# A gated dilated convolution on one core: another list of instructions, with one accumulating transfer fewer and four output evictions more on VectorE

## The chip, the cores and the metric

The kernel runs on one core of a Trainium2 chip. The metric is the device time of one execution in microseconds (us); the profile's span is the part of it between the first and the last recorded event of the core. Five engines work side by side and meet only through semaphores: TensorE multiplies matrices (PE in the profile, PEld for its weight loads), VectorE (DVE) and ScalarE (ACT) do elementwise work and can read the matrix products out of PSUM, GpSimd (POOL) does elementwise work on SBUF and issues transfers that add to what lies at their target, and SyncE (SP) issues the other transfers. Each engine takes its own instructions strictly in the order in which they were written.

## The reference

```python
x: (2, 16000, 256)   w: (3, 256, 512)   w_o: (256, 256)      # all bf16
xp = jnp.pad(x, ((0, 0), (4, 0), (0, 0)))                    # causal, dilation 2
h  = x @ w[0] + (x two steps back) @ w[1] + (x four steps back) @ w[2]
f, g = h[..., :256], h[..., 256:]
z  = jnp.tanh(f) * sigmoid(g)
return z @ w_o
```

So there is a convolution with three taps over time, a gate, and a projection.

## The kernel before

**Tiling.** Channels lie on the partitions. The 32000 time steps are cut into 23 groups. A group reads its piece of x through a transposing transfer into a tile `xt`, in which time is split into 4 or 6 phases, so that the dilation of two turns into neighbouring pairs of phases. There are three kinds. Group 0 (kind P) is computed straight from the taps, to have work while the rest is loaded. The four groups of kind B (4 phases) use the short-convolution trick that gets two pairs of outputs from four products instead of six; its operands are `m`, `p`, `d0`, `d3`, sums and differences of pairs of phases. The eighteen groups of kind A (6 phases) get three pairs of outputs from five products; their operands start as `u1`, `e`, `f`, `u0`, `u2` (each a sum or difference of pairs of phases), and four of them are finished by adding a multiple of `u1`: `rm` is e + `u3`, `rp` is f + `u1`, `r0` is u0 + `uh`, `ri` is u2 + `ud`, where `u3`, `uh`, `ud` are scaled copies of `u1`. An operand tile is 128 partitions by 1024 elements in bf16 (640 where the group has 160 rows).

**Blocks.** A block is one group with one quarter of the 512 outputs. There are 88, in the order of `ORDER`. A block of kind A runs: the first product (token `F`) into a PSUM bank `b`; ScalarE copies it to `ss` (`c`); the middle product is added (`M`); a copy of the bank scaled against `ss` goes to `hh`, on VectorE (`h`) or plainly on ScalarE (`k`); the last product is added (`L`); VectorE makes from `ss` and `b` the start of a second bank `a` (`A`) and, from `hh`, the middle pair `yy` (`Y`); two more products land on the banks (`Z` on `b`, `I` on `a`); ScalarE applies tanh or sigmoid to `b`, `yy` and `a` (`b`, `y`, `a`). Kind B has no `M`, `h`, `Y`. Bank `b` exists three times, bank `a` twice. All products of a block are two matmuls on line 359. When tanh and sigmoid of a half are there, VectorE multiplies them (`g`, lines 456 and 460), and the projection of 128 rows by two phases is four matmuls on line 478 (`P`). Its bank (three of them) is evicted to the output tile `osb` by ScalarE (`e`, line 495) or VectorE (`v`, line 487), and SyncE stores a finished `osb` (`s`). The pieces of the last group are projected in two halves (`H`, `R`).

**Who makes the operands.** A token such as `u2.10` names an operand and the number of its group. Bare, it is one VectorE instruction (line 330, or 328 for the scaled copies). With a `d` behind it, GpSimd issues a transfer that adds the scaled copy to the operand in place (line 325): an accumulating DMA of 256 KB. With a `q` and a number, it is a quarter of the operand as one GpSimd instruction of 256 elements per partition (160 for the narrow group); four such tokens make the operand. The number says behind which of VectorE's latest instructions the piece is held.

```python
if "q" in token:
    on_gpsimd(token)
elif token[-1] == "d":
    pre(*group_of(token[:-1]), None)
...
    note(pre(*group_of(token), nc.vector))
...
elif what in "ev":
    out_evict(*pieces[int(token[1:])], on_v=what == "v")
```

**What sets the order.** `PLAN` is one list of all tokens behind the start-up. The program walks it and writes every instruction to its engine's queue, without any reordering. An engine's order is therefore the order of its tokens in the list, and where a token of one engine stands between two tokens of another tells what is meant to start when. Waits follow from the data and from the buffers.

Of the kernel before, what the change touches and what calls it, by code (L numbers as in the profile page):

```python
# [34 lines left out]
A f.6q22 b P s11 uh.5 M a u2.5q82 Y F y rp.5d u0.5 P k16 Z e.6 e27 r0.5d L b g I c P u2.6q118 A y F M e28 u1.6q63 Y
P c f.6q1 h17 Z y I ud.5 e29 rm.5 M b s12 L h18 a u2.6q1 x F a P u2.6q45 A c L Y u1.6q20 e30 I A u1.6q108 e31 M Z a
Y u1.6q33 P k19 g ri.5d Z b L e32 u0.6 P f.7q89 y A I b F uh.6 u2.6q46 e33 P Y c F r0.6d u3.6 P y g rm.6d M e34 I
f.6q13 a h20 P c Z y u1.7 L f.6q67 b M A e35 P rp.6d Y F k21 s14 P a e.7 s13 Z c ud.6 I g e36 ri.6d L b M u2.7q71 A
e37 P a h22 F u0.7q137 e38 P Y u0.7q65 c L s15 Z y uh.7 x u2.7q72 A M b I f.7q90 h23 e39 F f.7q1 y Y L c f.7q114 I
v40 a Z u2.7q22 Y a M g P b P k24 A F e41 x L rp.7 e42 P c A Z y u1.8 I u0.8q93 b M Y a P u0.7q161 h25 Z y F uh.8 b  # L40
u3.7 I u2.8 s16 c rm.7d F e43 f.8 M c L g rp.8d k26 M a u2.7q76 A L k27 Y I y u0.8q1 A Z a u0.7q103 P v44 b u0.8q81
L Y y s17 P u0.8q162 A e45 F r0.7d e46 Z ud.7 Y c I ri.7d P b u3.8 r0.8d M u1.9 a Z e.8 k28 F b ud.8 L rm.8d e.9 c I
y g F u2.9q179 M y A P c P e47 h29 f.9q46 M a Y s18 f.9q43 L e48 s1 ri.8 u2.9q60 Z x k30 I A b L u2.9q117 Y a F y
u0.9q14 A Z c I g u0.9q1 b P a M Y F y u0.9q167 h31 I e49 ud.9 Z c u3.9 L b e.10 rm.9d M e50 A P u0.9q89 a F s19 h32
e51 I x Y f.9q75 c P g L a f.9q1 Z e52 Y P b M u0.10q72 A e53 F u1.10 Z c I h33 y P uh.9 b M f.10 s20 r0.9d y L h34
u2.9q136 F e54 A P a L c Y u0.10q111 I y Y u0.10q129 M e55 Z A rp.9d k35 P uh.10 ri.9d b Z g a I L e56 ud.10 u3.10 F
b s21 A P a x F u2.10 c P Y c M y u1.11 Z e57 M h36 b I u3.11 e58 L g u2.11q137 k37 F P a A L y Y u2.11q107 P c A
u2.11q42 Z y I f.11 rm.10d y M Y b u0.10q118 P e59 v60 rp.10d Z k38 s22 F uh.11 r0.10d b g P a L u0.11 c F P e61 A I
e62 ud.11 ri.10q1 M c Y P y r0.11d u1.12 Z y rp.11d M h39 b I e.11 e63 L u3.12 a F ri.10q1 h40 P e64 A P c ri.10q52
L e65 Y u2.11q33 M a s24 g ri.10q10 Z k41 x I b A L a F u2.12q103 Y y I u2.12q220 A c Z uh.12 rm.11d P y Y P b g M y  # L50
s23 F k42 v66 I u1.13q121 c Z v67 a ri.11d L f.12 e68 M b P A s25 e.13q152 P k43 x Y F a e.13q125 L c e.12 u1.13q170
Z e69 A I b M f.13 u1.13q1 e70 P Y a F u2.12q52 P v71 k44 Z c rp.12d g L y rm.12d M b A I k45 ud.12 P u2.13q69 Y a
s26 F e72 u0.12 L u2.13q15 c Z A P y u2.13q63 M Y b I u1.13q210 e73 h46 F a u2.12q15 Z c uh.13 rp.13d I g y L ri.12d
b M ud.13 P A k47 e.14q113 F a Y L c e.13q247 I A y Z e.14q191 e74 M Y e.13q189 P b h48 Z r0.12d y u3.13 F a g L
rm.13d b I f.14 c P u2.14q103 y F A e75 M v76 u0.13q202 I c h49 P u0.13q57 e77 M Y a u2.14q55 s28 L e78 h50 x
u0.13q102 Z a Y P u2.13q15 b L A e.14q70 y P y F u1.14 u0.13q101 Z A c I b ri.13d Y M e79 s27 F r0.13d u3.14 k51 g Z
c I u1.15 a L M b A f.15q131 P a u3.15 F f.15q226 e80 Y P k52 s29 e.15 P c x L g e81 Z y M A u0.15q78 b I h53
e.14q248 P y F Y e82 u2.15q170 L a u0.14 u2.15q128 Z c P Y b I u2.15q278 A e83 M rm.14d a ud.14 F h54 e84 Z rp.14d
uh.14 I c g L r0.14d b P e85 u2.14q287 A M y P Y e86 P h55 u2.14q38 y F u1.16 a Z ri.14d I g b L c P Y f.16q41 e87 F
e88 A M f.16q231 c P h56 u0.15q120 e89 Z v90 M a f.15q216 s32 L b s30 h57 u0.15q75 I x y A f.16q213 F a L Y f.15q45  # L60
y P uh.15 u0.15q94 c Z A e91 I s31 u2.15q110 Y M b P rm.15d g a F k58 rp.15d Z u3.16 c uh.16 L y u2.16 M b I ud.15 A
k59 P ri.15d F a ud.16 r0.15d Y L y P d0.3q55 c A Z e92 M Y b I u1.17 e93 d0.3q1 Z a h60 I m.3q93 b F e.16 ri.16d L
c g F rm.16d y P e.17q121 A c M e94 P h61 e95 M e.17q79 Y I a s34 f.16q22 L h62 s33 a Z A e96 d3.3q1 P y d0.3q64 Y P
e.17q45 b L g Z y rp.16d F b d3.3q40 Y I c P d3.3q65 A e97 F m.3q78 u0.16 e98 d0.3q252 M c I s35 h63 r0.16d Z a
u3.17 M e99 f.17 P b h64 L rp.17d a P A y u0.17q176 F e100 Y L y P d3.3q161 A u0.17q101 c Z Y I e.17q58 b I e101 g M
rm.17d a F s36 u2.17q5 h65 y P s4 s7 Z c g p.3q78 s5 L b M A e102 P u0.17q112 k66 Y F u2.17q17 a P v104 c L m.3q26
uh.17 p.3q67 Z e103 A M p.3q36 b s37 ud.17 I m.3q10 k67 Y P u0.17q286 a F v106 p.3q135 y L r0.17d Z c A P u2.17q16 y
M Y b I u2.17q30 e105 h68 Z a v107 F ri.17q5 b L ri.17q4 s38 y I A ri.17q3 P c Y F y ri.17q28 M c g Z a P h69 b P g
e108 M L e109 h70 F y I A c P a Y L I y Y Z a A M b P h71 y Z v110 F b L c I A F a L Y P c A I e113 v111 Z a L v112
Z b P A b s40 I g y s39 P a F I v114 c F P g c L a Z e115 A L P v116 b I e117 A Z s41 P g a s6 I b v118 Z a P b P  # L70
e119 g H P v120 s42 R P e121 H e123 v122 H R s44 R e124 s43 e125 s45
"""


# [572 lines left out]
```

## Time and profile before

| | |
|---|---|
| time, median of 3 runs | 258.87 us (258.47 to 259.78) |
| the profiled execution's own time | 258.77 us |
| its span | 256.6 us |
| TensorE busy | 249.9 us (97%), 1428 matmuls |
| VectorE busy | 242.8 us (95%), 405 instructions |
| ScalarE busy | 243.7 us (95%), 492 instructions |
| GpSimd busy | 176.9 us (69%), 249 instructions |

Each share of busy time says less than it seems. A matmul's recorded time reaches past the start of the next one, and so does that of a VectorE or ScalarE instruction: back to back, they start sooner after each other than each of them lasts. To see what an engine's work costs it, one has to read the distance between the starts of neighbours, and to see its waits, the places where that distance is longer than usual. The groups of instructions ("lines"), the chain of work that ended last, and the timeline in order of time are the views used below; a time at the start of a timeline row is us from the span's start, the second number is the us that the row lasts, and xN counts merged instructions.

### The profile page before, as it was taken

Reading aid. Unit: us, or ns where it says so; the run is one execution under the profiler, and the core shown is the slowest. Engines: PE = TensorE matmul, PEld = TensorE weight load, DVE = VectorE, ACT = ScalarE, POOL = GpSimd, SP = SyncE. Lnnn points to the kernel's source line nnn. Section 1 sums busy time; section 2 is a strip of 40 time slices with the busy share of each in tenths; the row PEclk is TensorE's granted clock in tenths of the full one; section 3 lists DMA queues with packets and bytes.
Section 4 is the critical chain, followed back from the end, with each engine's and each line's share of the span. In section 5 each row is a group of like instructions: output and inputs, shape, how many; then the busy total and the mean of one; then the engine's idle time right before and its main releaser. Section 6 shows DMA issues by size and latency. Waiting matters only on the chain.

```text
span 256.6 us, 4575 instructions
## 1 busy us (share of the span) xinstructions
PE 249.9 (97%) x1428; PEld 138.0 (54%) x1428; DVE 242.8 (95%) x405; ACT 243.7 (95%) x492; POOL 176.9 (69%) x249
## 2 busy tenths in 40 slices
PE   8999999999999999999999999999999999999992
PEld 4655555555555565545555555555555545555581
DVE  2999999999999999999999999999999999999991
ACT  4988999999999999999999999999999999999893
POOL 1064554997699888499764887999798798897000
PEclk9999999999999999999999999999999999999997
DMA  6999979989989899999999999996999998773054
GB/s 184 213 202 213 196 172 159 232 143 203 187 199 271 187 200 249 182 289 200 200 237 212 249 196 188 290 244 147 212 260 171 216 219 224 198 217 102 0 226 176
DMA packets 84320, 51.73 MB, mean 202 GB/s; under 512 B 69032, under 2 KB 70312, under 8 KB 84296
## 3 DMA queue, kind: packets, MB, share of 16 engines
q1 hardware_dynamic: 74168, 33.71, 54.3%
q0 software_dynamic: 9216, 16.78, 37.7%
q10 hardware_dynamic: 912, 0.95, 1.1%
q8 instruction: 11, 0.18, 0.3%
q14 instruction: 13, 0.11, 0.1%
HBM read 1.25 MB, written 16.38 MB: 69 GB/s over the span
## 4 chain that ended last, share of the span: by engine, by line
PE 82%; DVE 8%; DMA 3%; ACT 2%; issue 2%; ACTq 0%; DVEq 0%
PE b L359 48%; PE o_ps L478 18%; PE a L359 13%; DVE a L393 2%; DMA e<-u 2%; DVE zz L460 2%; DVE yy L393 2%; PE b L379 1%; PE a L379 1%; DMA xn<-in_x_dram 1%; DVE hh L393 1%; ACT osb L495 1%; ACT sg L441 1%; ACT th L441 0%; ACT ss L390 0%
## 5 line engine op out<-in xcount | busy, mean ns | idle before, releaser
L330 POOL TENSOR_TENSOR u<-xt 128x256 bf16<-128x256 bf16 x88 | 66.8, 774 | 15.0 <-PE b L359 8.4
L478 PE MATMUL o_ps<-wo_sb,zz 128*128 128x256 bf16 x496 | 72.0, 273 | 0.0
L495 ACT CAST osb<-o_ps 128x512 bf16<-128x512 f32 x101 | 63.8, 646 | 0.9 <-PE o_ps L478 0.7
L478 PEld LDWEIGHTS <-zz 128*128 128x128 bf16 x496 | 48.5, 98 | 27.6
L393 DVE SCALAR_TENSOR_TENSOR a<-ss,b 128x512 f32<-128x512 f32 (+1 forms) x88 | 59.5, 679 | 2.3 <-PE b L359 1.3
L390 ACT COPY ss<-b 128x512 f32<-128x512 f32 (+1 forms) x88 | 55.0, 628 | 0.9 <-PE b L359 0.6
L359 PEld LDWEIGHTS <-w_sb 128*128 128x128 bf16 x352 | 34.1, 97 | 35.1 <-issue 3.0
L359 PE MATMUL b<-e,wm_sb 128*128 128x512 bf16 x144 | 42.8, 379 | 0.3 <-DMA e<-u 0.3
L359 PE MATMUL b<-u,w_sb 128*128 128x512 bf16 x144 | 42.9, 379 | 0.2
L359 PE MATMUL b<-u,wa_sb 128*128 128x512 bf16 x144 | 42.9, 379 | 0.0
L359 PE MATMUL b<-f,wp_sb 128*128 128x512 bf16 x144 | 42.9, 379 | 0.0
L359 PE MATMUL a<-u,w_sb 128*128 128x512 bf16 x144 | 42.5, 379 | 0.3 <-DVE a L393 0.2
L460 DVE TENSOR_TENSOR zz<-th,sg 128x1536 bf16<-128x1536 bf16 (+2 forms) x46 | 41.3, 897 | 0.2
L441 ACT ACTIVATE th<-b 128x512 bf16<-128x512 f32 (+1 forms) x44 | 28.0, 636 | 1.4 <-ACT ss L390 0.7
L441 ACT ACTIVATE th<-a 128x512 bf16<-128x512 f32 (+1 forms) x44 | 28.6, 649 | 0.3 <-PE a L359 0.2
L441 ACT ACTIVATE sg<-b 128x512 bf16<-128x512 f32 (+1 forms) x44 | 28.0, 635 | 0.6 <-PE b L359 0.5
L441 ACT ACTIVATE sg<-a 128x512 bf16<-128x512 f32 (+1 forms) x44 | 28.3, 642 | 0.0
L359 PEld LDWEIGHTS <-wm_sb 128*128 128x128 bf16 x176 | 17.0, 98 | 17.2 <-DMA e<-u 1.2
L359 PEld LDWEIGHTS <-wp_sb 128*128 128x128 bf16 x176 | 16.9, 98 | 17.3 <-issue 1.6
L393 DVE SCALAR_TENSOR_TENSOR hh<-ss,b 128x512 f32<-128x512 f32 x38 | 25.9, 681 | 0.2
L393 DVE SCALAR_TENSOR_TENSOR yy<-hh,b 128x512 f32<-128x512 f32 x38 | 25.6, 678 | 0.0
L441 ACT ACTIVATE sg<-yy 128x512 bf16<-128x512 f32 x36 | 24.9, 693 | 0.7 <-DVE yy L393 0.7
(68 smaller groups left out, 373.2 us busy)
## 6 DMA issues: line engine op xcount, KB each, us to landing
out_dram<-osb SPq DMA_DIRECT2D x36, 384.0 KB, 3.5
u<-uh POOLq DMA_DIRECT2D x18, 256.0 KB, 4.8
f<-u POOLq DMA_DIRECT2D x16, 256.0 KB, 4.7
u<-ud POOLq DMA_DIRECT2D x15, 256.0 KB, 4.6
e<-u POOLq DMA_DIRECT2D x15, 256.0 KB, 4.8
out_dram<-osb SPq DMA_DIRECT2D x8, 256.0 KB, 3.1
w_sb<-in_w_dram ACTq DMA_DIRECT2D x3, 256.0 KB, 4.1
xt<-in_x_dram SPq DMA_TRANSPOSE x22, 8.0
```

The costliest lines, as they stand in the source:

```text
L330: ins = eng.tensor_tensor(out=o, in0=a, in1=b, op=op)
L359: nc.tensor.matmul(G[bank, oi][:, :2 * R], lhsT=wmat[:, ct, osl], rhs=G[mv][:, :, ct, :R], start=which == "first" and ct == 0, stop=ct == ...
L379: nc.tensor.matmul(G[bank, oi][:, :4 * r].rearrange("p (j r) -> p j r", j=4), lhsT=w_taps[tap][:, ct, osl], rhs=xt[:, j0:j0 + 4, ct, c0 + ...
L390: nc.scalar.copy(out=G["ss", oi][:, :n], in_=G["b", oi][:, :n])
L393: return note(nc.vector.scalar_tensor_tensor(out=out, in0=in0, scalar=scalar, in1=in1, op0=ALU.mult, op1=op))
L441: nc.scalar.activation(out=G[name, dt][:, j:j + 2, :R], in_=G[bank, oi][:, :2 * R].rearrange("p (q r) -> p q r", q=2), func=(ACT.Tanh, ACT ...
L460: note(nc.vector.tensor_tensor(out=G["z"][:, dt, :, :n], in0=G["th", dt][:, :, :n], in1=G["sg", dt][:, :, :n], op=ALU.mult))
L478: nc.tensor.matmul(o_ps[:, q, :], lhsT=z, rhs=wo_sb[:, dt, :], start=dt == 0 and (q == 0 or len(dts) == NT), stop=dt == NT - 1, skip_group ...
L495: copy(out=G["osb", at][:, 2 * jp:2 * jp + 2, :], in_=o_ps[:])
```

## The change

Only `PLAN` is changed, and all of it: 1730 tokens before and after, in another order, with these exchanges. Nothing else in the file differs, and the order of the blocks, of the groups and of each product kind is the same.

```diff
-m.0 d3.0 p.0 F F d0.0 c F c G L w L A c D wa.5q2 D A wa.2q5 Z d0.1 I b D m.1 a L wa.3q1 F d A wa.10q2 Z c p.1 I
+m.0 p.0 d3.0 F F d0.0 c D c D G L w L A D wa.5q2 F A wa.6q6 d I c d0.1 Z a m.1 Z b L G b I A wa.4q1 F a d3.1 F c Z
...
-e119 g H P v120 s42 R P e121 H e123 v122 H R s44 R e124 s43 e125 s45
+a Z s41 v118 I b P g a Z P v119 b P e120 g s42 P v121 H H e122 H R R s43 v123 R e124 v125 s44 s45
```

| what | before | after |
|---|---|---|
| output evictions on ScalarE / VectorE (`e` / `v`) | 103 / 23 | 99 / 27 |
| `hh` on VectorE / ScalarE (`h` / `k`) | 38 / 34 | 37 / 35 |
| accumulating transfers (`d`) | 64 | 63 |
| operand instructions on VectorE of line 330 | 74 | 75 |
| scaled copies on VectorE (`u3`, `uh`, `ud`) | 54 | 54 |
| quarter pieces on GpSimd (with the 16 of the weights, `wa`) | 176 | 176 |

Operand by operand: `u2.10` and `u2.16` go from VectorE to GpSimd; `d3.2`, `d0.3` and `d3.3` from GpSimd to VectorE (the last two belong to the narrow group); `ri.8` and `rp.7` from VectorE to a transfer; `rp.12` and `r0.0` from a transfer to VectorE; `rm.7` and `r0.17` from a transfer to GpSimd; `ri.17` from GpSimd to a transfer.

VectorE, where the third group of four phases (its `xt` is `xt_145`) is prepared, some 12 us behind the start of the list. Before:

```order
L330 TENSOR_TENSOR m_397<-xt_145 128x1024
L393 SCALAR_TENSOR_TENSOR a_407<-ss_352,b_345 128x512
L393 SCALAR_TENSOR_TENSOR a_416<-ss_389,b_376 128x512
L330 TENSOR_TENSOR u0_422<-xt_143 128x1024
L328 TENSOR_SCALAR u3_430<-u1_350 128x1024
L330 TENSOR_TENSOR u2_436<-xt_143 128x1024
L330 TENSOR_TENSOR p_440<-xt_145 128x1024
```

The same place in the changed list:

```order
L330 TENSOR_TENSOR d3_402<-xt_145 128x1024
L330 TENSOR_TENSOR m_411<-xt_145 128x1024
L330 TENSOR_TENSOR d0_422<-xt_145 128x1024
L393 SCALAR_TENSOR_TENSOR a_428<-ss_386,b_377 128x512
L393 SCALAR_TENSOR_TENSOR a_440<-ss_409,b_398 128x512
L328 TENSOR_SCALAR ud_451<-u1_361 128x1024
```

The difference `d3` of this group, four GpSimd pieces before, is now a VectorE instruction ahead of `m`, and `d0` has come up behind it.

GpSimd's last instructions, which make the last operands of the last group of six phases (u0, u2) and of the narrow group (m, p). Before:

```order
L330 TENSOR_TENSOR u0_3180<-xt_2697 128x256
L330 TENSOR_TENSOR p_3241<-xt_2886 128x160
L325 DMA u0_3180<-uh_3280 128x1024
L330 TENSOR_TENSOR u2_3224<-xt_2697 128x256 x2
L330 TENSOR_TENSOR u2_3224<-u2_3224,ud_3294 128x256 x4
```

After:

```order
L325 DMA u2_3161<-ud_3270 128x1024
L330 TENSOR_TENSOR u0_3210<-xt_2722 128x256
L330 TENSOR_TENSOR m_3282<-xt_2856 128x160
L330 TENSOR_TENSOR u0_3210<-xt_2722 128x256
L330 TENSOR_TENSOR u0_3210<-u0_3210,uh_3276 128x256 x4
```

The sum onto u2 (`ri.17`) has become a transfer, and the sum onto u0 (`r0.17`) four quarter pieces, the last work of GpSimd.

ScalarE's last instructions; `osb` and `odd` are output tiles, `th` and `sg` results of tanh and sigmoid. Before:

```order
L441 ACTIVATE sg4_3589<-b_3533 128x2x160
L495 CAST osb6_3564<-o_ps_3591 128x512
L495 CAST osb6_3612<-o_ps_3607 128x512
L493 CAST odd_3625<-o_ps_3605 128x256
L495 CAST osb4_3636<-o_ps_3622 128x512
L495 CAST osb4_3636<-o_ps_3628 128x512
```

After:

```order
L441 ACTIVATE sg4_3592<-a_3561 128x2x160
L441 ACTIVATE sg4_3592<-b_3536 128x2x160
L495 CAST osb6_3608<-o_ps_3596 128x512
L495 CAST osb6_3608<-o_ps_3613 128x512
L495 CAST osb4_3636<-o_ps_3621 128x512
```

The eviction of `odd` and the second one of `osb4` have left ScalarE. VectorE's last instructions, before:

```order
L487 CAST osb6_3564<-o_ps_3571 128x512
L456 TENSOR_TENSOR zo_3577<-th4_3580,sg4_3589 128x128
L460 TENSOR_TENSOR zz_3576<-th4_3580,sg4_3589 128x4x128
L487 CAST osb6_3612<-o_ps_3597 128x512
L487 CAST osb6_3612<-o_ps_3616 128x512
```

After:

```order
L456 TENSOR_TENSOR zo_3589<-th4_3574,sg4_3592 128x128
L460 TENSOR_TENSOR zz_3588<-th4_3574,sg4_3592 128x4x128
L487 CAST osb6_3608<-o_ps_3603 128x512
L487 CAST odd_3632<-o_ps_3619 128x256
L487 CAST osb4_3636<-o_ps_3625 128x512
```

So the last two evictions of all, one behind the other on ScalarE before, are now on two engines.

More of the change, by code (lines that the diff above doesn't have):

```diff
@@ new lines @@
+e10 rm.1 Z c f.3q18 A P b u1.3q12 M Y y F r0.1d g k4 Z c I e.2 b M a u2.2 L rm.2d e11 F h5 u1.3q6 e12 I A r0.2d P c
+u3.3 L a Y M y f.2 Z u0.3q1 e13 P A x b I g k6 u0.3q30 F a L Y c I f.3q30 A y P Z a f.3q46 Y M e14 rp.2d e.3 Z b
+ri.2d I ud.3 k7 v15 F b L u1.4 c F uh.3 y u0.3q1 P A a M u3.4 u0.3q32 c P Y P k8 rm.3d g y Z r0.3d L e18 v16 M b
+f.4q43 I A k9 F v17 a L f.3q70 c Y P s8 y u2.4q60 A Z y u2.4q5 I Y b M rp.3d e.4 e19 Z a F h10 rm.4d b I u2.3 L c
+u1.5 F x f.4q1 a M A c P g k11 e.5q65 M y L Y k12 P u2.4q3 A e20 I e21 L f.4q7 Y Z a ri.3d f.5 P b I u0.4 y Z
@@ new lines @@
+F y I u0.8q26 A c M e47 P Y f.9q43 e48 M s18 h29 a u2.9q86 x Z k30 L e.9 u0.9q32 b I A y L f.9q76 Y F a I g c u2.9q1
+Z e49 M A b P r0.8d h31 a P s17 u2.9q24 y Y F L e50 u1.10 Z c u2.9q170 s19 I A b M f.9q120 Y y P e51 f.9q93 h32 F y
+Z e.10 rp.9d L c u3.9 P b g rm.9d M a F u0.10q73 e52 h33 P c A I u0.9q36 e53 L Y a M u0.10q117 s20 Y e54 Z x
+u2.10q47 h34 y P u0.9q156 I b A L y g F a P c uh.9 Z u2.10q1 Y e55 M u0.9q113 b A I k35 P e.11 r0.9d y Z f.10 L a
+ud.9 F b A ri.9d I c u3.10 F rp.10d a Y M c P uh.10 e56 h36 Z e57 M g s21 I b x L k37 u1.11 u2.11q202 F a A P c L
@@ new lines @@
+e80 Z e81 I s29 u0.15q25 A P b x h53 P a u2.15q101 F Y e82 u2.14q72 L c P u0.15q136 Y e83 M u2.14q144 y A Z y
+u2.15q123 I h54 Z b rp.14d u0.14 L a g F b r0.14d I c f.15q226 Y F a P A c M u0.15q126 v84 y Z u2.14q105 y I h55 P b
+ri.14d u3.15 M u1.16 e85 F e86 g L c s31 P A f.16q308 k56 x P e87 ud.15 M f.16q283 Y a I e88 f.15q157 L h57 a Z
+u2.15q239 A L b u2.15q168 P s30 Y e89 F u0.15q166 v90 y Z f.16q155 c A P b I f.15q155 Y M y rm.15d g F k58 rp.15d I
+c u1.17 Z a L u0.16 b M A P k59 uh.15 F e91 d0.3 r0.15d L Y a P ri.15d c P A u2.16q18 y Z Y M e92 I b v93 s33
@@ L72 @@
+ri.17d e106 L u0.17q34 e107 Z A c P s38 m.3q64 Y b I u0.17q8 M y Z y r0.17q14 h68 I a r0.17q9 F b g L r0.17q27 c P
+e108 A F M r0.17q95 Y c I y h69 M a Z h70 P b g L y L a A F P Y c I A y Z Y M e109 I b h71 Z a v110 F b L c P A y F
+L Y c I e111 v112 P a Z v113 a L P A b s40 P A y s39 Z g F b I c P g a F I c v114 L a Z A L e115 P A b I e116 v117 P
+a Z s41 v118 I b P g a Z P v119 b P e120 g s42 P v121 H H e122 H R R s43 v123 R e124 v125 s44 s45
 """
```

79 lines of the change are left out of this document (31 added, 48 removed).

## The prediction, made before the changed kernel was run

> **What bounds the kernel now.** I read the first page and the chain of waits, then counted each engine's work by lines, then looked in the timeline at the places where TensorE starts late.
>
> ```profile
> span 256.6 us, 4575 instructions
> PE 249.9 (97%) x1428; PEld 138.0 (54%) x1428; DVE 242.8 (95%) x405; ACT 243.7 (95%) x492; POOL 176.9 (69%) x249
> PE 82%; DVE 8%; DMA 3%; ACT 2%; issue 2%; ACTq 0%; DVEq 0%
> ```
>
> The chain runs on TensorE for 82% of the span, and VectorE is next. TensorE's work is best told from the distance of its starts:
>
> ```profile
> 40.28 1.29 PE b L359 x6
> 46.04 0.87 PE o_ps L478 x8
> 11.20:251.70 240.50, 201.85 (x848) 81.99 (x848) 1.00 0.95 202
> 11.20:251.70 240.50, 72.42 (x500) 48.84 (x500) 1.00 0.95 202
> 11.30 1.46 PE L359 MATMUL b<-m,wm_sb 128*128 128x512 bf16 x6
> 250.20 1.47 PE L478 MATMUL o_ps<-wo_sb,zz 128*128 128x256 bf16 x12
> ```
>
> A product matmul costs 1.29/6 = 0.215 us in the chain, a projection matmul 0.87/8 = 0.109. The two window rows count them (the first is line 359, the second line 478): 848 x 0.215 = 182.3, less 32 narrow ones of 320 instead of 512 columns at, by their size, 0.08 less each, 2.6, plus 500 x 0.109 = 54.5, plus six matmuls of the start group, 0.8: 235.0 us. From 11.30 to 251.67 there are 240.4. So TensorE loses some 4 to 5 us in all behind its start. That is the most that a better list could win there, and what a worse one makes larger. Two of the losses:
>
> ```profile
> 110.86 0.59 PE L359 MATMUL b<-f,wp_sb 128*128 128x512 bf16 x2
> 110.89 0.69 DVE L393 SCALAR_TENSOR_TENSOR a<-ss,b 128x512 f32<-128x512 f32 x1
> 111.49 0.68 DVE L393 SCALAR_TENSOR_TENSOR yy<-hh,b 128x512 f32<-128x512 f32 x1
> 111.63 0.59 PE L359 MATMUL a<-u,w_sb 128*128 128x512 bf16 x2 [0.18 <-DVE a L393]
> 112.22 0.59 PE L359 MATMUL b<-u,w_sb 128*128 128x512 bf16 x2
> 201.43 5.33 DMA e<-u
> 205.88 0.59 PE L359 MATMUL b<-u,w_sb 128*128 128x512 bf16 x2
> 206.81 0.61 PE L359 MATMUL b<-e,wm_sb 128*128 128x512 bf16 x2 [0.34 <-DMA e<-u]
> ```
>
> Two product matmuls take 0.43, so the pair behind 110.86 was due at 111.29. It starts at 111.63, right when VectorE's `a` ends at 111.58; the next pair was due at 112.06 and starts at 112.22, when `yy` ends. The pair due at 206.31 starts at 206.81, because an accumulating transfer issued at 201.43 took 5.33. Late VectorE is the frequent case, a late transfer the large one.
>
> **VectorE's margin.** The same count for VectorE; the five window rows are lines 393, 330, 328, 460 and 487, in this order:
>
> ```profile
> 9.20:252.60 243.40, 127.76 (x198) 1.00 0.95 202
> 9.20:252.60 243.40, 50.57 (x74) 117.65 (x160) 1.00 0.95 202
> 9.20:252.60 243.40, 23.62 (x54) 1.00 0.95 202
> 9.20:252.60 243.40, 41.26 (x46) 1.00 0.95 202
> 9.20:252.60 243.40, 15.56 (x23) 1.00 0.95 202
> 9.23 0.69 DVE L330 TENSOR_TENSOR m<-xt 128x1024 bf16<-128x1024 bf16 x1
> 9.84 0.69 DVE L330 TENSOR_TENSOR d<-xt 128x1024 bf16<-128x1024 bf16 x1
> 22.81 0.42 DVE L328 TENSOR_SCALAR uh<-u 128x1024 bf16<-128x1024 bf16 x1
> 23.14 0.69 DVE L330 TENSOR_TENSOR m<-xt 128x1024 bf16<-128x1024 bf16 x1
> 23.75 1.28 DVE L393 SCALAR_TENSOR_TENSOR a<-ss,b 128x512 f32<-128x512 f32 x2
> 242.55 1.28 DVE L487 CAST osb<-o_ps 128x512 bf16<-128x512 f32 x2
> 244.15 0.95 DVE L460 TENSOR_TENSOR zz<-th,sg 128x1536 bf16<-128x1536 bf16 x1
> 245.02 0.68 DVE L487 CAST osb<-o_ps 128x512 bf16<-128x512 f32 x1
> 250.84 0.69 DVE L487 CAST osb<-o_ps 128x512 bf16<-128x512 f32 x1 [0.27 <-PE o_ps L478]
> ...
> L460 DVE TENSOR_TENSOR zz<-th,sg 128x1536 bf16<-128x1536 bf16 x36 | 35.5, 985 | 0.2
> ```
>
> Start to start, a sum of 1024 elements costs 9.84 - 9.23 = 0.61, a scaled copy 0.33, a step on a bank 1.28 - 0.69 = 0.60 (rounded), an eviction 1.28 - 0.68 = 0.60, a gate of 1536 elements 0.87. That gives 198 x 0.60 = 118.8, 74 x 0.61 = 45.1, 54 x 0.33 = 17.8, 46 gates of which 36 are large at 0.87 and ten smaller at about 0.5 by their size, 36.3, and 23 x 0.60 = 13.8: 231.8 us. From 9.23 to 251.53 there are 242.3. About 10.5 us, 4%, are waits and stretched instructions, and little of it is free in the middle:
>
> ```profile
> 53.00:105.00 52.00, 51.93 (x293) 28.43 (x292) 51.43 (x85) 51.94 (x106) 42.90 (x59) 1.00 0.99 207
> 105.00:157.00 52.00, 51.65 (x285) 27.48 (x284) 51.98 (x90) 51.77 (x104) 38.93 (x49) 1.00 1.09 214
> ```
>
> (Windows: length, then busy time of TensorE, its weight loads, VectorE, ScalarE, GpSimd.) VectorE is busy 51.43 and 51.98 of 52 us. It is a second bound, hardly behind TensorE.
>
> **The change part by part.** *VectorE's total.* Four evictions more, 4 x 0.60 = +2.4; one `hh` less, -0.6; one 1024-wide sum fewer (u2.10, u2.16, ri.8 and rp.7 go, d3.2, rp.12 and r0.0 come), -0.6; two narrow differences more (d0.3, d3.3, 640 elements: between the scaled copy's 0.33 and the full 0.61, I take 0.4, since it lies by size nearer to a third off), +0.8. Sum +2.0, bounds +1.9 to +2.4.
>
> *Where it lies.* I priced VectorE's tokens with these durations (unrounded, which makes the whole 231.1 instead of 231.8) and counted those that stand in each list ahead of the same amount of TensorE work behind its first product at 11.30:
>
> | TensorE work done, us | 43 | 85 | 92 | 139 | 199 | 210 | 229 | all |
> |---|---|---|---|---|---|---|---|---|
> | VectorE work ahead, before | 44.0 | 85.2 | 91.8 | 139.8 | 198.4 | 208.3 | 225.5 | 231.1 |
> | after | 44.6 | 86.7 | 93.3 | 139.7 | 198.8 | 209.3 | 226.3 | 233.1 |
>
> So 1.2 of the 2.0 us lie behind the last 7 us of TensorE's work, where evictions run beside ScalarE's; 0.8 lie ahead of it. At 85 to 92 us the changed list is 1.5 ahead, at 139 equal. With no idle time in the middle, VectorE's lateness passes to TensorE, as at 111. I take +0.8, what is ahead of 229 us; the bounds are 0 (all of it disappears in the 10.5 us) and +2.0 (nothing does).
>
> *The tail.* Before, the last two evictions follow each other on ScalarE:
>
> ```profile
> 251.49 1.07 ACT L495 CAST osb<-o_ps 128x512 bf16<-128x512 f32 x2 [0.34 <-PE o_ps L478]
> ```
>
> They end at 252.56, 0.89 behind TensorE's end at 251.67. After, the last one is on VectorE, behind the short `odd`, and should start with TensorE's end: 0.05 + 0.69 = 0.74. That saves 0.15; bounds -0.3 to +0.2 (a late `odd`).
>
> *ScalarE.* Four evictions fewer and one copy more: 3 x (1.07 - 0.60) = -1.4 us of work. The weight loads that it held up:
>
> ```profile
> PEld L359 <- ACT hh L403: 0.5, 2, 0.3
> PEld L359 <- ACT sg L441: 0.4, 1, 0.4
> ```
>
> That is 0.9 at most to win. I take -0.2, since the 1.4 us are spread over 240. Bounds 0 and -0.9.
>
> *Transfers.* One of 64 falls away, but the distance between issue and first reader is moved for all of them.
>
> ```profile
> u<-uh POOLq DMA_DIRECT2D x18, 256.0 KB, 4.8
> u<-ud POOLq DMA_DIRECT2D x15, 256.0 KB, 4.6
> ```
>
> The two kinds land 4.8 and 4.6 us behind their issue in the median. The late one at 206 (`rm.15`) had 4.3 us of TensorE work between its token and its reader, and has 4.8 now: its 0.5 us may be won back. But the shortest distance was 4.3 and is now 3.9, for `r0.1` and `ri.12`: if both take the median, they are 0.9 and 0.7 late. Of the three with 4.3 before only one came late, so I count half of the 1.6: +0.8 - 0.5 = +0.3; bounds -0.5 and +1.1.
>
> *GpSimd* keeps 176 pieces; eight narrow ones become wide. It is busy 69% and costed at nothing, except at its end (below).
>
> Sum: 0.8 - 0.15 - 0.2 + 0.3 = +0.75. On the profiled execution's 258.77 us (256.6 of span and 2.2 around) this is 259.5. The median of the runs is 258.87, 0.1 higher, so I forecast **259.6 us**.
>
> **Rivals.** *VectorE passes on all of it (slower).* If at 85 to 92 us, where its list is 1.5 ahead, TensorE is held for that long, and the later lateness comes on top, all +2.0 arrive: 258.87 + 2.0 - 0.15 - 0.2 + 0.3 = 260.8. It decides once VectorE has no gap left in 53 to 105 us. For it speaks 51.43 of 52 busy; against it, that the lists are level again at 139. The Trainium skill (Perfetto Trace Analysis, Optimizing Scalar/DVE Operations) says that with a saturated VectorE it may make sense to move work to ScalarE. This change moves work the other way, and by that rule this rival would be the likely one; the trace agrees that VectorE is full, but ScalarE is busy 95% as well.
>
> *GpSimd's last operand or a short transfer comes late (slower).* The four pieces that finish `r0.17` now stand at GpSimd's end, the last one 0.9 us of TensorE work ahead of its reader. Such four took
>
> ```profile
> 232.32 3.26 POOL L330 TENSOR_TENSOR u<-u,ud 128x256 bf16<-128x256 bf16 x4
> ```
>
> 3.26 us, 0.8 each, so 0.1 is left, where the last piece had 3.0 us of cover in the old list: GpSimd late by one piece holds TensorE for 0.7. With both short transfers late in full (+0.8 on the forecast's share) that makes 259.6 + 1.5; half of it falls into stalls that VectorE's lateness makes anyway: 260.4.
>
> *The list fits better (faster).* Lateness at 111, 206 and the like belongs to the old list's pairs of neighbours. If VectorE's more goes into its 10.5 us, `rm.15` arrives in time, ScalarE's 0.9 vanish: 258.87 - 0.5 - 0.9 - 0.15 = 257.3. For it speaks that TensorE's loss is all due to single places; against it, that VectorE gets fuller and that the shortest transfer gets shorter.
>
> *The list does not act as it reads.* Excluded: the built queues follow it word for word.
>
> **How the numbers follow.** Forecast 0.46, VectorE in full 0.22, GpSimd or transfers 0.12, faster 0.20. The forecast's own bounds, with not all ends at once, are 258.4 to 260.6. The range reaches to 257.7 below, and to 261.5 above for the two slower rivals with something on top. A change of less than 0.5% (1.3 us) can't be told from none here. Faster than 257.6 needs most of the last rival: 0.14. Slower than 260.2: most of the two slow rivals and a sixth of the forecast, 0.34. Within: 0.52.
>
> **What would show it.** VectorE's rows: 27 evictions, 233 us of starts, its busy share in 53 to 105 us at the full 52. TensorE's late starts: more of them behind `a`, `yy` and `hh`, above all between 60 and 110 us. The transfer of `rm.15` no longer in the chain, `r0.1` (a u<-uh near 47 us) or `ri.12` (a u<-ud near 175 us) in it if they are late. The last eviction on VectorE, ending 0.75 behind TensorE. The forecast is wrong if TensorE's loss falls below 4 us (the list was better than its VectorE load), or if it grows at the end of GpSimd's queue.

## The result, and the profile after

| | before | after |
|---|---|---|
| median, same chip and session | 258.74 us (258.30 to 260.42, 13 runs) | 259.87 us (259.13 to 261.23, 13 runs) |
| ratio after / before | | 1.0043, 95% interval 1.0024 to 1.0063 |
| profiled execution | 258.77 us, span 256.6 | 259.13 us, span 257.4 |

The change costs 1.13 us, 0.43%, and the interval leaves out 1. Times and ratios here and below leave out executions over 1.5% above the fastest of the same kernel; there was one of 268.61 us in experiment 1 and one of 266.39 in experiment 5. The first page of the kernel after, in the order in which the lines of before were shown (span; busy us of each engine; the chain by engine):

```profile
span 257.4 us, 4573 instructions
PE 249.6 (97%) x1428; PEld 137.8 (54%) x1428; DVE 245.0 (95%) x409; ACT 242.6 (94%) x489; POOL 177.0 (69%) x248
PE 83%; DVE 11%; issue 3%; POOL 1%; ACT 0%; DVEq 0%; ACTq 0%
```

VectorE has 2.2 us of busy time more, ScalarE 1.1 less, and the 3% of DMA have left the chain. Its rows by group (line, tiles, count, then busy us and mean ns of one) show the 27 evictions:

```profile
L487 DVE CAST osb<-o_ps 128x512 bf16<-128x512 f32 x26 | 17.6, 681 | 0.0
L487 DVE CAST odd<-o_ps 128x256 bf16<-128x256 f32 x1 | 0.4, 423 | 0.3 <-PE o_ps L478 0.3
```

The profiled execution of after was the fastest of its 13, and its TensorE began its first wide product at 10.84 us, before's at 11.30. So I compare what TensorE loses behind that start: the distance from the end of that first matmul to the end of the last one, 240.00 us before and 241.01 after, less 235.9. The 235.9 are the same matmuls as the prediction's 235.0, at the distances that most of them have in these two traces, 0.216, 0.136 and 0.109 us for 512, 320 and 256 columns; the prediction rounded the first to 0.215. The loss is 4.07 us before and 5.08 after, +1.01. To see whose it is, I take every TensorE start that is over 0.05 us later than its predecessor's shape explains, and put it down to the operand, copy or buffer that was ready last. Where two were ready within some 0.05 us of each other the choice between them is open, which can move 0.1 us between two columns:

| late starts, us, put down to | VectorE | ScalarE | transfers | GpSimd | sum | loss |
|---|---|---|---|---|---|---|
| before | 2.38 | 0.81 | 0.68 | 0 | 3.87 | 4.07 |
| after | 2.59 | 1.99 | 0 | 0 | 4.59 | 5.08 |

VectorE's total hardly changes, but its places do: between 60 and 110 us its late starts go from 0.36 to 1.42 us, between 110 and 160 from 1.56 to 0.26, and behind 220 from 0.26 to 0.86.

The two largest single ones are new. The first, in the timeline of the kernel after (start, us that it lasts, engine, and in brackets the idle time ahead and what ended it):

```profile
114.98 0.59 PE L359 MATMUL a<-u,w_sb 128*128 128x512 bf16 x2
115.05 0.58 ACT L495 CAST osb<-o_ps 128x512 bf16<-128x512 f32 x1 [0.68 <-DMA out_dram<-osb]
115.53 0.59 ACT L390 COPY ss<-b 128x512 f32<-128x512 f32 x1
116.17 0.60 PE L359 MATMUL b<-e,wm_sb 128*128 128x512 bf16 x2 [0.59 <-ACT ss L390]
```

TensorE's pair at 114.98 should be followed at 115.41 and is followed at 116.17, 0.76 late. It waits for ScalarE's copy, which stands behind an eviction that waited 0.68 for a store to free its output tile: the stores of two earlier tiles (`s14`, `s15`) stand later in the new list. The second, on VectorE and then TensorE:

```profile
224.60 1.17 DVE L460 TENSOR_TENSOR zz<-th,sg 128x1536 bf16<-128x1536 bf16 x1
225.69 0.78 DVE L330 TENSOR_TENSOR d<-xt 128x640 bf16<-128x640 bf16 x1
226.39 0.50 DVE L328 TENSOR_SCALAR ud<-u 128x1024 bf16<-128x1024 bf16 x1
226.81 0.98 DVE L328 TENSOR_SCALAR uh<-u 128x1024 bf16<-128x1024 bf16 x1
227.71 0.68 DVE L487 CAST osb<-o_ps 128x512 bf16<-128x512 f32 x1
228.31 0.68 DVE L393 SCALAR_TENSOR_TENSOR a<-ss,b 128x512 f32<-128x512 f32 x1
228.91 0.67 DVE L393 SCALAR_TENSOR_TENSOR hh<-ss,b 128x512 f32<-128x512 f32 x1
229.64 0.59 PE L359 MATMUL b<-f,wp_sb 128*128 128x512 bf16 x2 [0.60 <-DVE hh L393]
```

Seven VectorE instructions run back to back, with `d3.3` (the 640-wide difference that came over from GpSimd) and an eviction among them; the last one, `hh`, holds TensorE for 0.76. Four of the seven also last longer than elsewhere in this trace, by some 1.1 us in all: `zz` 1.17 instead of 0.95, `d3.3` 0.78 instead of the 0.48 of `d0.3`, `ud` 0.50 and `uh` 0.98 instead of 0.42. GpSimd works beside them:

```profile
224.98 1.13 POOL L330 TENSOR_TENSOR p<-xt 128x160 bf16<-128x160 bf16 x1
226.67 0.82 POOL L330 TENSOR_TENSOR p<-xt 128x160 bf16<-128x160 bf16 x1
```

So this late start has two parts, the work that was put in and the stretching; no run takes the second away alone. The tail is as forecast:

```profile
251.62 0.60 PE L478 MATMUL o_ps<-wo_sb,zz 128*128 128x256 bf16 x4
252.26 0.69 DVE L487 CAST osb<-o_ps 128x512 bf16<-128x512 f32 x1
```

TensorE ends at 252.22, VectorE's last eviction at 252.95, 0.73 behind; before it was 0.89.

### The profile page after: what moved, and what is told of

Same layout as the page of the kernel before. It is cut to its first block, busy times and chain, and to the rows that moved or that the text cites. A ratio compares the mean times of both kernels' runs of the same rounds, so it can differ in the third digit from the quotient of the medians.

```text
span 257.4 us, 4573 instructions
## 1 busy us (share of the span) xinstructions
PE 249.6 (97%) x1428; PEld 137.8 (54%) x1428; DVE 245.0 (95%) x409; ACT 242.6 (94%) x489; POOL 177.0 (69%) x248
## 4 chain that ended last, share of the span: by engine, by line
PE 83%; DVE 11%; issue 3%; POOL 1%; ACT 0%; DVEq 0%; ACTq 0%
PE b L359 48%; PE o_ps L478 18%; PE a L359 12%; DVE a L393 3%; DVE yy L393 2%; DVE zz L460 1%; PE b L379 1%; PE a L379 1%; DVE e L330 1%; PE a L149 1%; DVE osb L487 1%; DVE hh L393 1%; DVE u L330 1%; DVE uh L328 0%; POOL e L325 0%
## 5 line engine op out<-in xcount | busy, mean ns | idle before, releaser
L330 POOL TENSOR_TENSOR u<-xt 128x256 bf16<-128x256 bf16 x96 | 72.2, 768 | 8.2 <-PE a L359 2.0
L495 ACT CAST osb<-o_ps 128x512 bf16<-128x512 f32 x98 | 59.6, 634 | 1.3 <-DMA out_dram<-osb 0.7
L390 ACT COPY ss<-b 128x512 f32<-128x512 f32 (+1 forms) x88 | 54.2, 618 | 0.8 <-PE b L359 0.8
L460 DVE TENSOR_TENSOR zz<-th,sg 128x1536 bf16<-128x1536 bf16 (+2 forms) x46 | 40.7, 886 | 0.0
L441 ACT ACTIVATE th<-a 128x512 bf16<-128x512 f32 (+1 forms) x44 | 27.8, 631 | 1.2 <-PE a L359 1.1
L393 DVE SCALAR_TENSOR_TENSOR hh<-ss,b 128x512 f32<-128x512 f32 x37 | 25.0, 678 | 0.6 <-PE b L359 0.4
L330 POOL TENSOR_TENSOR f<-xt 128x256 bf16<-128x256 bf16 x28 | 20.8, 750 | 6.1 <-PE b L359 5.6
L393 DVE SCALAR_TENSOR_TENSOR yy<-hh,b 128x512 f32<-128x512 f32 x37 | 24.5, 676 | 0.2 <-PE b L359 0.2
```

The source lines that it names most:

```text
L330: ins = eng.tensor_tensor(out=o, in0=a, in1=b, op=op)
L390: nc.scalar.copy(out=G["ss", oi][:, :n], in_=G["b", oi][:, :n])
L393: return note(nc.vector.scalar_tensor_tensor(out=out, in0=in0, scalar=scalar, in1=in1, op0=ALU.mult, op1=op))
L441: nc.scalar.activation(out=G[name, dt][:, j:j + 2, :R], in_=G[bank, oi][:, :2 * R].rearrange("p (q r) -> p q r", q=2), func=(ACT.Tanh, ACT ...
L460: note(nc.vector.tensor_tensor(out=G["z"][:, dt, :, :n], in0=G["th", dt][:, :, :n], in1=G["sg", dt][:, :, :n], op=ALU.mult))
L495: copy(out=G["osb", at][:, 2 * jp:2 * jp + 2, :], in_=o_ps[:])
```

## The experiments

Ratios are to before on the same chip and in the same session; before had 258.78 us beside experiments 1 to 4, 258.74 beside 5 to 8, 259.00 beside 9 to 12. "Loss" and "late" are counted as in the table above, from one profiled execution each. In experiments 1 to 4 the ratios lie 0.14 to 0.18% below the ratios of the two medians, so a gain or loss there is known to some 0.4 us only. Where a VectorE instruction is moved or taken out (4, 7, 8), the numbers behind `q` of pieces between its two places point at a neighbouring VectorE instruction; this side effect isn't separated.

### 1 and 2. Shorter evictions on VectorE, in both lists

```diff
-            copy(out=G["osb", at][:, 2 * jp:2 * jp + 2, :], in_=o_ps[:])
+            if on_v:
+                note(nc.vector.memset(G["osb", at][:, 2 * jp:2 * jp + 2, :], 0.0))
+            else:
+                copy(out=G["osb", at][:, 2 * jp:2 * jp + 2, :], in_=o_ps[:])
```

> The changed kernel; its 26 evictions on VectorE that go to the wide output tiles are replaced by fills with zero of the same tiles, so those parts of the output are left out; the PSUM bank is then not read. If VectorE's load is what holds TensorE (theory V), some 26 x (0.60 - 0.2 to 0.35) = 6 to 10 us of VectorE work go, the 2.5 us that TensorE starts late behind a, yy, hh in the changed kernel vanish for the most part, and the time falls from 259.9 to 257.0 to 258.0. If the loss comes from single late places of another kind, a store that frees an output tile late, transfers, GpSimd (theory S), it stays within 0.7 of 259.9.

> The same on the kernel before: its 23 evictions on VectorE become fills, those parts of the output are left out. Theory V: the 2.4 us that TensorE starts late behind VectorE go for the most part, 256.4 to 257.2, and the two kernels so shortened lie closer to each other than 1.1 us. Theory S: the kernel before stays at 258.7 and the difference of 1.1 between the two lists stays.

Measured: 259.43 us for the changed list (ratio 1.0009, 0.9985 to 1.0034) and 258.89 for the old one (0.9986, 0.9963 to 1.0010). The rows of the two kernels:

```profile
L496 DVE MEMSET osb<- 128x256 uint32 x26 | 7.1, 272 | 0.4
```

```profile
L496 DVE MEMSET osb<- 128x256 uint32 x23 | 6.3, 272 | 0.3
```

Each eviction is 0.41 us shorter (681 to 272 ns), some 10 us of VectorE work in all. By the medians 0.4 us is won in the changed list and none in the old one; by the ratios 0.9 and 0.4. In the old list VectorE still accounts for 2.27 us of late starts. In the changed list its late starts do fall, from 2.59 to 1.2, those at 65 us wholly and the one at 229.6 by half; but those of ScalarE grow by some 0.5, GpSimd's last pieces cost 0.4, and the sum goes only from 4.59 to 4.0. The difference between the two lists is 0.5 by the medians, which is neither theory V's picture nor the unchanged 1.1 of theory S. The reading that VectorE's *total* passes to TensorE falls here: in the old list the evictions stand where VectorE can wait anyway, and in the changed one others take back most of what its shorter evictions give.

### 3. The stores s14 and s15 earlier

```diff
-... c s4 A Z y s14 u3.7 M s15 y u0.8q154 ...
+... Y e35 s14 I c u3.6 ...    ... Y I e38 s15 P c ...
```

> The changed kernel with two of its stores (s14, s15) issued right behind the last eviction of their tiles instead of about 10 and 7 us later. Theory S: the wait of 0.68 us of a ScalarE eviction for a store at 114.4 us, and the 0.76 us that TensorE starts late at 116.2 behind it, vanish; the time falls by 0.5 to 0.8, to about 259.2. Theory V: the wait vanishes, but VectorE is as late soon after, and no more than 0.3 is won.

Measured: 259.55 us (1.0016, 0.9994 to 1.0038), 0.3 less than the changed list by the medians and 0.7 by the ratios, within the noise of both. The eviction no longer waits and the late start at 116 is gone, but the sum of late starts went only from 4.59 to 4.53: VectorE's went from 2.59 to 3.36. New ones stand at 121.7, 129.3, 132.9 and 155.4. One of them, `yy` and `hh` back to back ahead of a pair due at 121.51:

```profile
120.38 0.69 DVE L393 SCALAR_TENSOR_TENSOR yy<-hh,a 128x512 f32<-128x512 f32 x1
120.99 0.68 DVE L393 SCALAR_TENSOR_TENSOR hh<-ss,b 128x512 f32<-128x512 f32 x1
```

```profile
121.30 0.38 PE L359 MATMUL b<-u,w_sb 128*128 128x512 bf16 x1
121.72 0.59 PE L359 MATMUL b<-f,wp_sb 128*128 128x512 bf16 x2
```

### 4. d3.3 back on GpSimd

```diff
-... M e103 I d3.3 k66 F ...
+four pieces d3.3q1, behind u2.17q135, u2.17q61, u2.17q97 and u0.17q1
```

> The changed kernel with the narrow difference d3.3 taken from VectorE (0.70 us there in the profile, at 225.7) and put as four quarter pieces on GpSimd some 5 us earlier, where GpSimd has gaps. Theory V (load, or VectorE's and GpSimd's instructions stretching each other near 225 us): TensorE's late start of 0.76 at 229.6 behind hh shrinks to below 0.3, the time falls by 0.4 to 0.7. If that late start is only one of many that follow each other, nothing is won.

Measured: 261.53 us (1.0091, 1.0058 to 1.0124), 1.7 slower than the changed list. The late start at 229.6 is gone, and the last rival of the prediction is there in its place: GpSimd's four pieces that finish `r0.17` hold TensorE for 1.01 and 1.17 us at 238.6 and 240.0. GpSimd has four pieces more to make here, so this alone doesn't tell who was covering for whom. In that execution, the slowest of the nine, two transfers were late too, `ri.12` by 1.38 and `ri.17` by 0.42.

### 5. Four evictions from VectorE to ScalarE

```diff
-v39   v58   v74   v93
+e39   e58   e74   e93        (each at its place in the changed list; GpSimd's pieces stay held behind the same VectorE instructions)
```

> Four evictions of the changed list (v39, v58, v74, v93) go from VectorE to ScalarE in place; the list is otherwise the changed one. Theory L (load: the share of VectorE's total that a list carries passes to TensorE, as the forecast had it with 0.8 of 2.0): VectorE loses 4 x 0.60 = 2.4 us, TensorE gets about 1.0 back, 258.6. Theory B (bursts: VectorE cannot run ahead, it waits for products, so only the work between its last such wait and a late place counts): none of these four stands in the run of VectorE instructions ahead of a place where TensorE starts over 0.15 late (65.2, 96.9, 229.6), so nothing is won: 259.6, within 0.3, with the same late places; ScalarE gets 4 x 0.47 = 1.9 us, which can only lose.

Measured: 262.35 us (1.0148, 1.0107 to 1.0189), 2.5 us slower than the changed list. Both theories miss. VectorE's late starts stay at 2.5 to 2.6, though it has 2.4 us less to do: as theory B says, nothing is won there. ScalarE's go from 1.99 to 3.29, and four transfers come late (1.70 in all), the largest one in the timeline of TensorE:

```profile
193.36 0.61 PE L359 MATMUL a<-u,w_sb 128*128 128x512 bf16 x2 [0.99 <-DMA u<-ud]
```

So ScalarE has no room either: 1.9 us of work on it cost 1.3 us of late starts behind ScalarE alone. Why the transfers were late in this execution isn't shown.

### 6. Four evictions from ScalarE to VectorE, in the old list

```diff
-e29   e58   e74   e93
+v29   v58   v74   v93        (each at its place in the old list; GpSimd's pieces stay held behind the same VectorE instructions)
```

> Four evictions of the old list (e29, e58, e74, e93) go from ScalarE to VectorE in place: the one part of the change that its count names, alone. Theory L: VectorE gets 4 x 0.60 = 2.4 us, 0.4 of it passes: 258.8 + 1.0 = 259.8. Theory B: it costs only where one of the four stands in the run ahead of a place that is late or nearly so, at most 0.3 us each; ScalarE's late bank of 0.125 at 86.2, behind e29, goes. 258.8 to 259.3.

Measured: 260.77 us (1.0078, 1.0053 to 1.0103), 2.0 slower, twice what theory L said and more than B. VectorE's late starts go from 2.38 to 4.84. Each of the four shows; the last one, on VectorE and TensorE:

```profile
208.50 0.69 DVE L330 TENSOR_TENSOR u<-xt 128x1024 bf16<-128x1024 bf16 x1
209.11 0.68 DVE L487 CAST osb<-o_ps 128x512 bf16<-128x512 f32 x1
209.70 0.68 DVE L393 SCALAR_TENSOR_TENSOR hh<-ss,b 128x512 f32<-128x512 f32 x1
```

```profile
209.12 0.59 PE L359 MATMUL b<-u,wa_sb 128*128 128x512 bf16 x2
210.44 0.61 PE L359 MATMUL b<-f,wp_sb 128*128 128x512 bf16 x2 [0.72 <-DVE hh L393]
```

The eviction stands right ahead of the `hh` that TensorE needs, which is 0.88 late. An eviction put in at a place of an already full order costs 2.0 / 4 = 0.5 us on average.

### 7. d3.3 earlier on VectorE

```diff
-... e91 d0.3 r0.15d ...        ... I d3.3 k66 F ...
+... e91 d0.3 d3.3 r0.15d ...   ... I k66 F ...
```

> One VectorE instruction, the narrow difference d3.3 (0.4 us, 0.7 as stretched), is moved from 225.7 us to right behind d0.3 (about 200 us), where TensorE had no late start over 0.1 us; VectorE's total stays. Theory L: no change, 259.6. Theory B: the late start of 0.757 at 229.6, behind hh (h67), ends a run of seven VectorE instructions back to back and falls to 0.1 or less; the time falls by 0.4 to 0.7, to 258.9 to 259.2.

Measured: 260.16 us (1.0057, 1.0038 to 1.0077), not faster. The late start at 229.6 is gone as theory B has it, and GpSimd's end is late in its place; its pieces and TensorE's reader of them:

```profile
232.71 1.34 POOL L330 TENSOR_TENSOR u<-xt 128x256 bf16<-128x256 bf16 x1
234.01 2.55 POOL L330 TENSOR_TENSOR u<-u,uh 128x256 bf16<-128x256 bf16 x4
```

```profile
235.98 0.38 PE L359 MATMUL b<-u,w_sb 128*128 128x512 bf16 x1 [0.30 <-POOL u L330]
236.61 0.38 PE L359 MATMUL b<-u,w_sb 128*128 128x512 bf16 x1 [0.25 <-POOL u L330]
```

They cost 0.46 and 0.41. In the changed list itself the same pieces and their reader are:

```profile
232.61 3.27 POOL L330 TENSOR_TENSOR u<-u,uh 128x256 bf16<-128x256 bf16 x4
235.69 0.62 PE L359 MATMUL b<-u,w_sb 128*128 128x512 bf16 x2
```

The last piece ends at 235.88, and the second matmul, which needs it, starts at 235.93, 0.03 late: there was no room left. VectorE's 0.76 at 229.6 had been covering for GpSimd: whoever was late first gave the other its time.

### 8. Four moves at once

```diff
-e.4 ... h10          c u1.7 P r0.6d          (s14, s15, d3.3 as in 3 and 7)
+h10 e.4              u3.6 Z g u1.7 e36
```

> The changed list with four places mended and no instruction changed: d3.3 behind d0.3; the sum e.4 behind h10 instead of ahead of it (late start of 0.375 at 65.2); u1.7 behind the gate instead of ahead of h20 (0.451 + 0.158 at 96.9); the stores s14 and s15 right behind their last evictions (0.758 at 116.2). Theory L: the same load on every engine, 259.6, within 0.3. Theory B: 2.5 us of late starts go; the stores alone won only some 0.1 because VectorE was late next, so I count half of their 0.758 and of the others two thirds: 257.9 to 258.4, which would be faster than before.

Measured: 261.20 us (1.0085, 1.0064 to 1.0107), 1.3 slower where theory B had it 1.5 to 2 faster. All four late starts are gone, and the moved `u1.7` made a worse one; VectorE, GpSimd and TensorE there:

```profile
97.75 0.94 DVE L328 TENSOR_SCALAR u<-u 128x1024 bf16<-128x1024 bf16 x1
98.61 0.94 DVE L460 TENSOR_TENSOR zz<-th,sg 128x1536 bf16<-128x1536 bf16 x1
99.48 1.61 DVE L330 TENSOR_TENSOR u<-xt 128x1024 bf16<-128x1024 bf16 x1
101.02 0.68 DVE L393 SCALAR_TENSOR_TENSOR a<-ss,b 128x512 f32<-128x512 f32 x1
```

```profile
99.60 3.99 POOL L330 TENSOR_TENSOR u<-xt 128x256 bf16<-128x256 bf16 x5
```

```profile
101.75 0.59 PE L359 MATMUL a<-u,w_sb 128*128 128x512 bf16 x2 [1.41 <-DVE a L393]
```

`u1.7` took 1.61 us, where the same sum takes 0.69 alone, with GpSimd's pieces beside it; the step on the bank behind it kept its 0.68. The fourteen traces bear this out: none of the 652 sums of 1024 elements without a GpSimd piece beside them took over 0.70 us, while of the 259 that had one beside them for more than half of their time 83 took over 0.75; of the 984 steps that make `a` over 512 columns with such a neighbour none took over 0.70. The numbers behind the `q` are there, by a remark in the kernel, to put GpSimd's pieces beside VectorE's steps on PSUM, and a sum that is moved can land among them.

### 9 to 11. VectorE relieved throughout

```diff
+    n //= 2
     stt(G["hh", oi][:, :n], G["ss", oi][:, :n], 1.5, G["b", oi][:, :n], ALU.subtract)
...
-                stt(G["y", oi][:, :n], G["hh", oi][:, :n], 2.0, b)
+                two = lambda t: t.rearrange("p (t m) -> p t m", t=2)
+                stt(two(G["y", oi][:, :n]), G["hh", oi][:, :n // 2].unsqueeze(1).to_broadcast([P, 2, n // 2]), 2.0, two(b))
```

> The old list with VectorE relieved throughout: each of its 38 copies hh (token h) computes half of its columns, and the step that makes yy reads that half twice, so half of the values of yy are not the reference's; order, waits and every other instruction stay. I estimate 0.3 us less for each, 11 us of VectorE work in all, in nearly every run of VectorE instructions. Expected where VectorE sets late starts of TensorE: most of the 2.3 us behind a, yy and hh go, 256.8 to 257.6. If such places are made by single waits that no lighter VectorE mends: 258.3 to 258.8.

> The same relief for the changed list, 37 copies. Theory L (the 1.1 us that the change costs are VectorE's additional load): with 11 us of room the additional load no longer passes; the difference to the old list with the same relief falls to 0.3 or less. Theory S (by the count of late starts the change adds 0.2 behind VectorE, 1.4 behind ScalarE, half of that the copy c that stands behind a held eviction at 116, and takes 0.7 off the transfers): the difference stays at 0.8 to 1.3, with the late start of 0.76 at 116 in place: 257.7 to 258.6.

> The kernel before this one with the stores s14 and s15 right behind their last evictions. Alone, that move took the late start of 0.758 away and won only 0.1 to 0.3, since VectorE was late next. If VectorE was indeed what took it back, the move now wins 0.6 to 0.8 against after_half_h. If something else takes it back (the end of GpSimd's work, ScalarE): 0.3 or less.

Measured: the old list 259.57 us (1.0021, 0.9995 to 1.0046), the changed one 259.85 (1.0033, 1.0013 to 1.0052), the changed one with early stores 258.52 (0.9987, 0.9962 to 1.0012). Each `hh` takes 0.26 less, in the rows of the old list:

```profile
L393 DVE SCALAR_TENSOR_TENSOR hh<-ss,b 128x256 f32<-128x256 f32 x38 | 15.8, 416 | 3.1 <-PE b L359 2.7 <-ACT th L443 0.2
```

| late starts, us | VectorE | ScalarE | transfers | GpSimd | sum |
|---|---|---|---|---|---|
| old list, relieved | 1.01 | 1.36 | 2.72 | 0 | 5.09 |
| changed list, relieved | 0.87 | 2.18 | 1.96 | 0.26 | 5.27 |
| changed list, relieved, early stores | 1.09 | 1.56 | 0.30 | 0.28 | 3.23 |

VectorE's late starts fall to less than half in both lists, and still neither kernel is faster: transfers come late instead. The largest one in the old list is the one that finishes `r0.17`, issued at 230.72 (it took 4.0 us, against 3.3 in the other four profiled executions of the old list), in the changed one `ri.12`, issued at 174.68; each with its reader on TensorE:

```profile
230.72 0.83 POOL L325 DMA_DIRECT2D u<-uh  x1
```

```profile
234.88 0.59 PE L359 MATMUL b<-u,w_sb 128*128 128x512 bf16 x2 [1.58 <-DMA u<-uh]
```

```profile
174.68 1.03 POOL L325 DMA_DIRECT2D u<-ud  x1
```

```profile
180.31 0.60 PE L359 MATMUL a<-u,w_sb 128*128 128x512 bf16 x2 [1.49 <-DMA u<-ud]
```

The difference of the two lists fell to 0.3 us, the number of theory L. The table doesn't bear out its reason: ScalarE's 0.74 at 116 stayed, as theory S had it, ScalarE's late starts are still 0.8 more in the changed list, and it is 0.8 less of late transfers that makes up for them. As these transfers vary between executions, the two theories aren't told apart here. The early stores, worth 0.3 alone by the medians, are worth 1.3 here, more than the 0.6 to 0.8 expected; in the two profiled executions `ri.12`, which took 5.58 us in the one and 4.08 in the other, is part of that. That VectorE took back what the early stores won in 3 is supported, not measured cleanly.

### 12. rm.15 earlier, in the old list

```diff
-uh.15 u0.15q94 c Z A e91 I s31 u2.15q110 Y M b P rm.15d g a
+uh.15 rm.15d u0.15q94 c Z A e91 I s31 u2.15q110 Y M b P g a
```

> The old list with one transfer, the one that finishes rm.15, issued about 1.7 us of TensorE work earlier (right behind uh.15, ahead of two pieces of u0.15 on GpSimd); nothing else moved. The forecast took 0.5 us for its late start. If it is won: 258.2 to 258.4, with no late start near 206.8. If VectorE or ScalarE are late next there, as at the other places that were mended: 258.6 to 258.9.

Measured: 258.42 us (0.9982, 0.9963 to 1.0001), 0.6 less than before by the medians, as if all of it were won; the interval just takes in 1. The issue on GpSimd and the reader on TensorE:

```profile
199.82 0.83 POOL L325 DMA_DIRECT2D e<-u  x1
```

```profile
206.09 0.59 PE L359 MATMUL b<-e,wm_sb 128*128 128x512 bf16 x2
```

The transfer took 6.20 us this time and was still in time by 0.07. The trace gives less than the medians: the sum of late starts goes from 3.87 to 3.67 only, because VectorE is late next, with a new late start of 0.26 behind `hh` at 208.5. Of the kernels that leave nothing out it has the lowest median, below both lists.

## Why the prediction was right, and which terms were not

The forecast was 259.6 us and +0.75; measured were 259.87 and +1.13. The sum held, but by terms that missed in both directions, so that its closeness is partly luck. The total loss of "some 4 to 5 us" that the prediction starts from is 5.4 by its own figures (240.4 - 235.0) and 4.1 at the distances used above.

- **VectorE, +0.8 of 2.0: mis-sized as it shows in the trace.** Late starts behind VectorE grew by 2.59 - 2.38 = 0.2. The places were right: 1.06 us more between 60 and 110 us, among them 0.45 and 0.16 at 97 us, where some 85 us of TensorE's work are done and the list is 1.5 ahead. What the prediction left out is that the old list's own late places between 110 and 160 us went away with its order, 1.3 us, before 0.6 came at the end. The step "VectorE's lateness passes to TensorE" is right where work is put in: 2.4 us in the old list cost 2.0 (experiment 6). What fails is the pricing by totals: some 10 us of evictions taken away won 0.9 us at most (1 and 2), 2.4 us taken away elsewhere left VectorE's late starts as they were (5), and one eviction put in cost 0.5.
- **ScalarE, -0.2: wrong in sign.** It has three instructions fewer in balance and yet 1.2 us more of late starts, 0.76 of them at 116. The failed step is that ScalarE's term was priced by its work alone. The stores `s14` and `s15` were not counted among the moved steps; one of their tiles holds an eviction, and the eviction holds the copy behind it. Experiment 3 shows the cause of the 0.76, and that mending it alone wins little; the other 0.4 are spread over small late starts.
- **Transfers, +0.3: -0.7 in the profiled execution.** `rm.15` is in time, as forecast (experiment 12 prices it at 0.6 by the medians and 0.2 in the trace). `r0.1` was not late: it took 3.3 to 3.4 us, not the median's 4.8, and landed 0.9 to 1.0 us ahead of its reader in all nine kernels with the changed list. `ri.12` is as short as forecast: its reader starts within 0.15 us of its landing in all nine; in two of them it took 5.4 and 5.6 us instead of 4 and held TensorE for 1.4 and 1.7. So this price is paid in some executions, which the profiled one of after didn't show. The term took each kind's median, but a transfer's time goes by its place: the 887 accumulating transfers of the fourteen traces took 3.3 to 11.4 us, and the `f<-u` issued near 81 us took 10.0 to 11.4 in all nine kernels with the changed list, without holding TensorE.
- **The tail, -0.15: measured -0.16.**
- **Sum.** 0.2 + 1.2 - 0.7 - 0.15 = 0.55 from the late starts over 0.05 us. TensorE's whole loss grew by 1.01, so 0.3 are in shorter ones; 1.01 - 0.16 = 0.85 against 1.13 in the medians. What is left of some 0.3 isn't placed; `ri.12` and the start (below) differ between executions by more than that. In the profiled executions the first wide product began at 11.50 us on average with the changed list and at 11.10 with the old one; if the timed runs are alike, this covers it, which isn't shown.

Of the rivals, "VectorE passes on all of it" is what experiment 6 looks like, and isn't what the searched list did. "GpSimd's last operand" was one step behind: in after it was not late because VectorE's 0.76 at 229.6 came first, and it appeared as soon as that was taken away (7, 8). "The list fits better" won its `rm.15` and lost it at the stores.

The Trainium skill's advice for a saturated VectorE (Perfetto Trace Analysis, Optimizing Scalar/DVE Operations), weighed in the prediction, is not borne out here: moving four evictions to ScalarE, which was 94% busy, cost 2.5 us.

## What to carry to other kernels

On this list, with three engines all over 90% busy, what TensorE lost was not a sum of loads but a set of single late places, and one often covered for the next: price an edit by the instruction that stands behind it and by who waits for that, and expect a mended place to give back most of its gain a few microseconds later. Work put into such an order cost most of its length (2.0 of 2.4 us), while work taken out won little (0.9 of some 10 us at most), so what an old list lost is no guide to what a new one will. No single mend gave back the 1.1 us of the change; relief of VectorE and the early stores together did, in a kernel whose values are not all the reference's (11). When steps move, count the stores that free buffers too, and keep a transfer's distance to its reader above the longest time that it takes at its place, not the median of its kind.

## What the hardware showed that I had not expected

**Half-rate matmuls at the start.** TensorE's instructions up to the first wide product are the same in all fourteen kernels, yet that product began between 10.84 and 11.91 us. Part of it is in the first 18 matmuls of 320 columns; in before, and in the kernel with four moves:

```profile
5.22 2.63 PE L379 MATMUL b<-xt,w_sb 128*128 128x320 bf16 x18
```

```profile
5.01 3.45 PE L379 MATMUL b<-xt,w_sb 128*128 128x320 bf16 x18
```

In the second the first seven start 0.22 to 0.27 us apart, the others 0.14. Two to seven such matmuls, worth 0.2 to 0.8 us, were in seven of the nine profiled executions with the changed list (not in that of after itself) and in none of the five with the old one. The windows read a granted clock of 1.00 there too, but the trace's record of that clock begins only where the slow starts end: at 4.71 us in before and at 6.73 in the kernel with four moves, between 3.49 and 6.73 over the fourteen. The Trainium skill (TensorE: Matmul & The Clock Gate, Part 1) describes a clock gate that runs TensorE at half rate until it has been busy for some 3.4 us, at a point that varies between runs; the factor of two agrees with it, and TensorE's work began at 0.78 us, 2.7 to 6.0 us ahead of the full rate. Why the two lists should differ, and whether they do in the timed runs, stays open.

**GpSimd beside VectorE.** A sum over SBUF took 1.61 us instead of 0.69 and a scaled copy 0.94 instead of 0.42 beside GpSimd's pieces, while steps that read PSUM kept their 0.68 (experiment 8). The Trainium skill (SBUF — State Buffer, Who interferes with whom) says that VectorE and GpSimd share a pair of ports, which VectorE's instructions with two SBUF inputs or in a two-port mode need; the rows agree. So these two engines don't meet only through semaphores.
